# A chunked scan with a gated feed-forward layer on one core: fewer dummy matmuls, a block's outputs in two steps, first block's splitting after the second block's attention

## The chip, the core and the metric

The kernel runs on one core of a Trainium2 chip. The core has a matmul engine (TensorE; in the profile PE for its matmuls and PEld for its weight loads) and three engines that work on whole tiles: VectorE (DVE), ScalarE (ACT) and GpSimd (POOL). SyncE (SP) starts the DMA transfers here. Each engine runs its own list of instructions in order and waits on semaphores for the others. Matmuls read SBUF, the on-chip memory, and write PSUM, which has eight banks; DVE and ACT read PSUM and write back to SBUF. The metric is the device time of one execution in microseconds (us), the median of several.

## What is computed

Attention with a decay over 768 positions in 4 batches and 8 heads, in chunks, with a state carried from chunk to chunk; its output, as 3,072 tokens of 256 features, goes through a gated feed-forward layer of width 1,536.

```python
for c in range(nc):
    cum = np.cumsum(la, axis=-1)
    L = np.exp(cum[:, :, :, None] - cum[:, :, None, :]) * causal
    y_intra = np.einsum('bhij,bhjd->bhid', (Cc @ Bc^T) * L, xc)
    y_inter = np.einsum('bhin,bhnd->bhid', Cc, state) * np.exp(cum)[:, :, :, None]
    y[:, :, sl] = y_intra + y_inter
    state = decay_full[:, :, None, None] * state + np.sum(Bx, axis=2)
...
g = x @ w_gate
silu = g * (1.0 / (1.0 + np.exp(-g)))
val = x @ w_val
return (silu * val @ w_out)
```

## The kernel before

The 768 positions are cut into six blocks of 128 (k = 0 to 5), and each block into two pieces of 64. A block of all four batches is 512 tokens, the width of one PSUM bank and of the large matmuls.

**Attention of a block.** The decays of a block are loaded into `L` and `E` and turned into products by scans on DVE (`scan_j`, `scan_n`; for three batches of block 0 the rows are first spread over the partitions by TensorE, tiles `a0_0` to `a2_1`). DVE weighs `xb` (`weigh_b`) and, late, `bc` (`weigh_c`). TensorE forms the sums of each piece (`sums`, tiles `st`) and the scores (`scores`, tiles `S`). DVE multiplies scores and decays (`mix`, which writes `L`; its steps are named ("M", k, p)) and steps the states (`T`). `outputs` then forms the block's result in four PSUM banks `y`: for each batch `values` (16 matmuls y<-L,xb) and `carried` (8 matmuls y<-bc,T). In the trace each such f32 matmul is two records with two weight loads. Block 0 has its own order: `values` for all batches in two groups, then `carried`.

**Feed-forward of a block.** For each f of 12 slices of the width, `gate_val` gives the gate (m = 0) and the value (m = 1), tiles `gv`; ACT takes the silu of the gate into `sg`, DVE multiplies it by the value (`product`), the result is split into a high and a low half (`hh` by `hid_high`, `hl` by `hid_low`), and `project` adds it to two banks `po`, which are copied out and stored. Block 0 uses unsplit f32 copies (`xf`) and unsplit weights for its `gv`: two matmuls each, four records. From block 1 on x and the weights are split into halves too (`xh`, `xl`; `wg0h`, `wg0l`, ...), six matmuls each.

**Weights.** They arrive as 64-bit numbers. Each of 18 pieces (12 of gate and value, `wg`, 6 of the output, `wo`) goes through `w_magnitude`, `w_range`, `w_rest`, `w_shift`, `w_sign` and `w_round` on ACT and DVE. The rounded f32 weight (the trace's CUSTOM_DVE write to `wg0w`) serves block 0. `w_high` and `w_low` split it for the later blocks.

**Dummies.** `idle` issues three bf16 matmuls of a tile of ones by itself into a spare bank, `rest0` or `rest1`. The list `IDLE` (L856) has one number for each call, its rank, in two groups: 23 calls in the first and 24 in the second, whose first call needs block 0's first mix.

**What sets the order.** Nothing is issued in the order of the code. `add` enters each step with an engine or a choice of engines, a cost, a rank (when it is due), what it needs, which buffers it takes and uses, and what it gives. `Plan.order` then simulates the engines with these costs and issues, each time, a step that can start first, and among those the one with the lowest rank. `Plan.clocked` lets planned matmuls take twice as long in a window of 3.4133 us when the window before it had less than 1.28 us of matmuls. The order that comes out is fixed in the program. At run time an engine never passes a waiting instruction, so a step planned too early holds what stands behind it, and a dummy is run whether or not it is needed. The order's buffers bind as well: four PSUM banks for `gv` and `po`, four for attention and dummies, 21 tiles `sg` (shared by the rounded `wg` weights and the products), four raw weight tiles, and one each of `L`, `E`, `bc`, `xb`.

In the code before, the outputs of a block are one step, added at L801:

```python
add("PE", 3.2, do(outputs, k), z + 11, need, takes=[("at", i) for i in y], uses=[L, *uses], gives=("y", k), kind="f", slack=SLACK)
```

`w_high` is added at L715 and `hid_high` at L833. Since all operations pass through a helper, the profile puts them on L192; its tile names tell them apart.

Of the kernel before, what the change touches and what calls it, by code (L numbers as in the profile page):

```python
# [17 lines left out]
BATCH, H, S, D, N = 4, 8, 768, 32, 16  # L18
# [9 lines left out]
NP = H // 2  # L28
NF = DFF // P
# [13 lines left out]
class Plan:  # L43
# [6 lines left out]
    WINDOW, AWAKE = 3.4133, 1.28  # L50
# [12 lines left out]
    def add(self, engine, cost, run, rank, needs=(), takes=(), uses=(), gives=None, kind=None, lag=0.0, rows=1.0, slack=0.0):  # L63
        engines = [(engine, cost)] if cost is not None else engine
        self.ops.append(Op(engines, run, rank, needs, takes, uses, gives, kind, lag, rows, slack))
# [37 lines left out]
    def clocked(self, t, cost, rows):  # L103

        while cost > 1e-9:
            w = int(t / self.WINDOW + 1e-9)
            rate = 1.0 if self.active.get(w - 1, 0.0) >= self.AWAKE else 0.5
            d = min(cost / rate, (w + 1) * self.WINDOW - t)
            self.active[w] = self.active.get(w, 0.0) + d * rate * rows
            cost -= d * rate  # L110
            t += d
        return t
# [90 lines left out]
def scan_moe_kernel(ctx: ExitStack, tc, aj, an, bc, xb, wgv, wo, cst, sel, out):  # L203
# [279 lines left out]
    def outputs(k):  # L483
        for b in range(BATCH):
            values(k, (b,), (0, 1))
            carried(k, b)
# [179 lines left out]
    def do(f, *a):  # L666
        return lambda *e: f(*a, *e)
# [4 lines left out]
        dict(SP=5.2, Act=3.0, DVE=1.0, PE=1.5, Pool=2.0, **{"-": 0.7}),  # L672
    )
    add = plan.add
# [29 lines left out]
    for i in range(NW):  # L704
# [10 lines left out]
        add([("Act", 0.6), ("DVE", 0.36)], None, do(w_high, i), r - 2.7, [("round", i)], gives=("wh", i))  # L715
# [9 lines left out]
    for k in range(NB):  # L725
        r = due(k)
# [19 lines left out]
        if not k:  # L746
# [14 lines left out]
            add("DVE", 0.35, clip_n, -1.4, ["an"], gives="clip_n")  # L761
            add("DVE", 1.17, do(scan_n, 0), -1.3, ["clip_n"], gives=("E", 0))
# [36 lines left out]
        if k:  # L799
            need = [*(("M", k, p) for p in range(NP)), ("ce", k), *steps]  # L800
            add("PE", 3.2, do(outputs, k), z + 11, need, takes=[("at", i) for i in y], uses=[L, *uses], gives=("y", k), kind="f", slack=SLACK)  # L801
# [14 lines left out]
    for k in range(NB):  # L816
        xs = [(t, k, i) for t in ("xh", "xl") for i in range(2 * K)]
        for f in range(NF):
# [14 lines left out]
            add([("Act", 0.6), ("DVE", 0.36)], None, do(hid_high, k, f), r, [("pr", k, f)], takes=[("hh", h)], uses=[t], gives=("hh", k, f))  # L833
# [22 lines left out]
IDLE = [-9.0] * 8 + [-3.8, -3.3, -2.8] + [-1.2 + 0.1 * i for i in range(12)], [15.0 + 0.5 * i for i in range(24)]  # L856
# [56 lines left out]
```

## Time and profile before

| | us |
|---|---|
| median of 3 runs | 369.84 |
| lowest, highest | 366.42, 373.3 |
| the profiled execution | 368.33 |
| its span, first to last instruction | 366.6 |
| mean granted TensorE clock in it | 0.995 |

The span is 1.7 us shorter than the time of the execution it belongs to. Three views of the profile are used further down. The chain of work that ended last starts from the last instruction and goes back, at each step, to what released it; its rows give start, length and tile, and "issue" is time in which the engine waited for nothing that the profile shows. The timeline lists what each engine ran, with the wait before it in brackets. The windows give each engine's busy time and instruction count in a stretch, with the granted clock and the DMA rate. A matmul's recorded duration overlaps its neighbours', so lengths of a stage are taken from start to start.

### The profile page before, as it was taken

The page shows a single profiled execution, that of the slowest core. Times are in us where ns is not written, and L with a number is a line of the kernel's source. Part 1 is how long each engine was busy: PE and PEld are TensorE (multiplying, and loading weights), DVE is VectorE, ACT ScalarE, POOL GpSimd, SP SyncE. Part 2 cuts the span into 40 slices and gives each one's busy share as a digit, 9 for nine tenths or more (in the row PEclk, how much of TensorE's full clock was granted, in tenths as well). Part 3 has the DMA queues.
Part 4 walks back from the last instruction along what each step waited for, and adds up shares of the span by engine and source line. Part 5 has one row for each costly group of instructions (what it writes and reads, how often), then busy time and mean ns, then how long its engine had stood idle before and what let it go on. Part 6 is the DMA issues. An engine that isn't in the chain of part 4 may idle for free.

```text
span 366.6 us, 7587 instructions
## 1 busy us (share of the span) xinstructions
PE 357.5 (98%) x3293; PEld 276.0 (75%) x3293; DVE 231.0 (63%) x409; ACT 127.0 (35%) x225; POOL 0.8 (0%) x6
## 2 busy tenths in 40 slices
PE   8989999999999999999999999899999899999996
PEld 6855445488877888877788877688878688888895
DVE  3899999989999693663367554359345334352241
ACT  3275684444234543121342221323312133221242
POOL 0000000000000000000000000000000000000000
PEclk9999999999999999999999999899999999999999
DMA  6749742880101921000550000570100000100001
GB/s 181 283 134 285 240 146 87 237 224 2 58 2 46 207 95 59 0 3 2 172 119 25 35 2 2 143 148 2 57 0 3 4 0 2 57 0 2 0 0 59
DMA packets 8737, 28.62 MB, mean 78 GB/s; under 512 B 1008, under 2 KB 1912, under 8 KB 8064
## 3 DMA queue, kind: packets, MB, share of 16 engines
q1 hardware_dynamic: 8704, 28.14, 26.3%
q8 instruction: 26, 0.43, 0.5%
q14 instruction: 7, 0.06, 0.0%
HBM read 24.79 MB, written 3.35 MB: 77 GB/s over the span
## 4 chain that ended last, share of the span: by engine, by line
PE 94%; DVE 3%; issue 2%; ACT 0%; ACTq 0%
PE gv L192 55%; PE po L192 27%; PE y L192 5%; PE rest L192 3%; PE S L192 2%; PE a L192 1%; PE st L192 1%; DVE L L192 1%; DVE wo4w L192 0%; DVE sg L192 0%; DVE wo3w L192 0%; DVE wo4l L192 0%; DVE wo3l L192 0%; ACT wo5w L192 0%; ACT wo4w L192 0%
## 5 line engine op out<-in xcount | busy, mean ns | idle before, releaser
L192 DVE TENSOR_TENSOR sg<-gv,sg 128x512 f32<-128x512 f32 x72 | 49.4, 687 | 83.0 <-PE gv L192 80.6
L192 ACT ACTIVATE sg<-gv 128x512 f32<-128x512 f32 x72 | 42.9, 596 | 108.8 <-PE gv L192 108.6
L192 DVE TENSOR_TENSOR hl<-sg,hh 128x512 fp32r<-128x512 f32 x72 | 48.6, 685 | 17.5 <-ACT hh L192 17.0
L192 ACT CAST hh<-sg 128x512 fp32r<-128x512 f32 x56 | 34.9, 622 | 46.1 <-PE po L192 35.6
L192 DVE TENSOR_TENSOR_SCAN L<-L,dj 128x520 f32<-128x520 f32 x21 | 25.8, 1233 | 1.0 <-DMA L<-clipped 1.0
L192 DVE TENSOR_TENSOR L<-S,L 128x512 f32<-128x512 f32 x24 | 15.4, 682 | 2.2 <-PE S L192 2.2
L192 PEld LDWEIGHTS <-unit 128*128 128x128 bf16 x141 | 11.5, 122 | 4.9 <-issue 3.7
L192 PE MATMUL y<-L,xb 64*32 64x64 f32 x768 | 11.7, 223 | 3.2 <-issue 3.2
L192 ACT COPY ob<-po 128x512 f32<-128x512 f32 (+1 forms) x13 | 7.2, 555 | 21.3 <-PE po L192 20.8
L192 PE MATMUL rest<-unit 128*128 128x128 bf16 x141 | 12.9, 263 | 1.0 <-DVE warm L192 1.0
L192 PEld LDWEIGHTS y<-L,xb 64*32 64x32 f32 x768 | 7.6, 105 | 5.8 <-issue 3.9
L192 PE MATMUL y<-bc,T 32*64 32x64 f32 x352 | 10.2, 229 | 1.2 <-issue 1.2
L192 PEld LDWEIGHTS y<-bc,T 32*64 32x64 f32 x352 | 7.2, 131 | 4.5 <-issue 2.7
L192 PE MATMUL po<-hh,wo0h 128*128 128x512 f32 (+1 forms) x26 | 9.9, 382 | 0.0
L192 DVE CAST xh<-y 128x256 fp32r<-128x256 f32 x8 | 3.0, 418 | 10.9 <-PE y L192 10.9
L192 PE MATMUL po<-hh,wo2h 128*128 128x512 f32 (+1 forms) x26 | 9.8, 378 | 0.0
L192 PE MATMUL po<-hl,wo5h 128*128 128x512 f32 (+1 forms) x26 | 9.8, 377 | 0.0
L192 ACT CAST xh<-y 128x256 fp32r<-128x256 f32 x12 | 3.8, 379 | 17.1 <-PE y L192 17.1
L192 PE MATMUL po<-hl,wo0h 128*128 128x512 f32 (+1 forms) x26 | 9.7, 374 | 0.0
L192 PE MATMUL po<-hh,wo1h 128*128 128x512 f32 (+1 forms) x26 | 9.7, 373 | 0.0
L192 PE MATMUL po<-hl,wo3h 128*128 128x512 f32 (+1 forms) x26 | 9.7, 373 | 0.0
L192 PE MATMUL po<-hh,wo0l 128*128 128x512 f32 (+1 forms) x26 | 9.7, 373 | 0.0
(285 smaller groups left out, 800.5 us busy)
## 6 DMA issues: line engine op xcount, KB each, us to landing
L<-clipped SPq DMA_DIRECT2D x10, 520.0 KB
xb<-in_xb SPq DMA_DIRECT2D x6, 768.0 KB, 12.0
bc<-in_bc SPq DMA_DIRECT2D x6, 512.0 KB, 3.8
out<-ob SPq DMA_DIRECT2D x11, 256.0 KB, 2.2
E<-clipped SPq DMA_DIRECT2D x5, 260.0 KB
wg0r<-in_wgv SPq DMA_DIRECT2D x1, 512.0 KB
wg1r<-in_wgv SPq DMA_DIRECT2D x1, 512.0 KB
wg2r<-in_wgv SPq DMA_DIRECT2D x1, 512.0 KB, 9.9
```

The costliest lines, as they stand in the source:

```text
L192: ins = getattr(self.engine, name)(*a, **k)
```

## The change

There are four edits.

1. `IDLE` keeps 8 calls (24 matmuls) ahead of everything and 14 (42 matmuls) for gaps, with a rank of 1000: they are planned only where nothing else could start. 141 dummies become 66.
2. The outputs of blocks 1 to 5 are two steps of two batches each. Between them stands a step on an engine that exists only in the plan, "~", with a cost of 2.6, so that the plan puts other matmuls there. The first half takes the four banks, the second gives the block's result and frees its buffers.
3. For block 0, `hid_high`, and for the twelve `wg` weights `w_high`, need the last mix of block 1, ("M", 1, NP - 1). Low halves follow high halves, so they move too.
4. Inside the plan, matmuls ahead of 17 us always count as slow, and the ranks of `clip_n` and `scan_n` of block 0 are later.

```diff
-    WINDOW, AWAKE = 3.4133, 1.28
+    WINDOW, AWAKE, COLD = 3.4133, 1.28, 17.0
...
-            rate = 1.0 if self.active.get(w - 1, 0.0) >= self.AWAKE else 0.5
+            rate = 1.0 if t >= self.COLD and self.active.get(w - 1, 0.0) >= self.AWAKE else 0.5
...
-    def outputs(k):
-        for b in range(BATCH):
+    def outputs(k, bs):
+        for b in bs:
             values(k, (b,), (0, 1))
             carried(k, b)
...
-        add([("Act", 0.6), ("DVE", 0.36)], None, do(w_high, i), r - 2.7, [("round", i)], gives=("wh", i))
+        later = [("M", 1, NP - 1)] if i < NF else []
+        add([("Act", 0.6), ("DVE", 0.36)], None, do(w_high, i), r - 2.7, [("round", i), *later], gives=("wh", i))
...
-            add("DVE", 0.35, clip_n, -1.4, ["an"], gives="clip_n")
-            add("DVE", 1.17, do(scan_n, 0), -1.3, ["clip_n"], gives=("E", 0))
+            add("DVE", 0.35, clip_n, -1.15, ["an"], gives="clip_n")
+            add("DVE", 1.17, do(scan_n, 0), -1.12, ["clip_n"], gives=("E", 0))
...
-            add("PE", 3.2, do(outputs, k), z + 11, need, takes=[("at", i) for i in y], uses=[L, *uses], gives=("y", k), kind="f", slack=SLACK)
+            add("PE", 1.6, do(outputs, k, (0, 1)), z + 11, need, takes=[("at", i) for i in y], uses=y, gives=("y", k, 0), kind="f", slack=min(k - 0.5, 2.5))
+            add("~", 2.6, lambda: None, z, [("y", k, 0)], gives=("pause", k))
+            add("PE", 1.6, do(outputs, k, (2, 3)), z + 11, [("pause", k)], uses=[L, *uses], gives=("y", k), kind="f")
...
-            add([("Act", 0.6), ("DVE", 0.36)], None, do(hid_high, k, f), r, [("pr", k, f)], takes=[("hh", h)], uses=[t], gives=("hh", k, f))
+            add([("Act", 0.6), ("DVE", 0.36)], None, do(hid_high, k, f), r, [("pr", k, f)] + ([] if k else [("M", 1, NP - 1)]), takes=[("hh", h)], uses=[t], gives=("hh", k, f))
...
-IDLE = [-9.0] * 8 + [-3.8, -3.3, -2.8] + [-1.2 + 0.1 * i for i in range(12)], [15.0 + 0.5 * i for i in range(24)]
+IDLE = [-9.0] * 8, [1000.0] * 14
```

Three places of the resulting order follow. The first is TensorE's list behind the first 24 dummies, in the front of the program (`a0_0` and so on are the spread decay rows, `unit` the tile of ones), before:

```order
L192 MATMUL a0_0_138<-rows_86,pick_82 128x260
L192 MATMUL a0_1_140<-rows_86,pick_82 128x260
L192 MATMUL a1_0_146<-rows_86,pick_82 128x260
L192 LDWEIGHTS unit_81
L192 MATMUL rest0_110<-unit_81 128x128
```

and now:

```order
L192 MATMUL a0_0_138<-rows_86,pick_82 128x260
L192 MATMUL a0_1_143<-rows_86,pick_82 128x260
L192 MATMUL a1_0_151<-rows_86,pick_82 128x260
L192 MATMUL a1_1_159<-rows_86,pick_82 128x260
L192 MATMUL a2_0_161<-rows_86,pick_82 128x260
L192 MATMUL a2_1_165<-rows_86,pick_82 128x260
L192 MATMUL S0_0_169<-Cz0_140,bc0_92 64x128
L192 MATMUL S0_1_170<-Cz0_140,bc0_92 64x128
```

The nine dummies in the middle of the a are gone, and so are the 36 between the scores and the sums of block 0; scores, sums, values and carried part now follow one another. Then 21 dummies stand ahead of the first gv (27 before), none between gv0_0 and gv0_3 (45 before), 9 ahead of gv0_7 and 12 ahead of block 1's scores.

The second place is TensorE's list around the outputs of block 3 (y3_0 to y3_3 are its four banks), before, from the end of the fourth batch:

```order
L192 MATMUL y3_2_1967<-bc3_1488,T3_1494 64x64
L192 MATMUL y3_3_1968<-bc3_1488,T3_1494 64x64
L192 MATMUL gv2_9_0_2066<-xh2_979,wg9h_887 128x512 x2
L192 MATMUL gv2_9_0_2066<-xh2_979,wg9l_966 128x512 x2
L192 MATMUL gv2_9_0_2066<-xl2_980,wg9h_887 128x512 x2
L192 MATMUL gv2_9_1_2086<-xh2_979,wg9h_887 128x512 x2
L192 MATMUL gv2_9_1_2086<-xh2_979,wg9l_966 128x512 x2
L192 MATMUL gv2_9_1_2086<-xl2_980,wg9h_887 128x512 x2
L192 MATMUL gv2_10_0_2100<-xh2_979,wg10h_909 128x512 x2
```

and now, from the end of the second batch:

```order
L192 MATMUL y3_2_1892<-bc3_1433,T3_1439 64x64
L192 MATMUL y3_3_1893<-bc3_1433,T3_1439 64x64
L192 MATMUL gv2_9_0_1943<-xh2_889,wg9h_836 128x512 x2
L192 MATMUL gv2_9_0_1943<-xh2_889,wg9l_894 128x512 x2
L192 MATMUL gv2_9_0_1943<-xl2_890,wg9h_836 128x512 x2
L192 MATMUL gv2_9_1_1950<-xh2_889,wg9h_836 128x512 x2
L192 MATMUL gv2_9_1_1950<-xh2_889,wg9l_894 128x512 x2
L192 MATMUL gv2_9_1_1950<-xl2_890,wg9h_836 128x512 x2
L192 MATMUL y3_0_1890<-L3_1437,xb3_1458 32x64
L192 MATMUL y3_2_1892<-L3_1437,xb3_1458 32x64
```

The twelve matmuls of gv2_9 stood behind all four batches and now stand between the second and the third. Blocks 4 and 5 read alike; in block 1 the pair gv0_10 stands there, in block 2 the projections of f = 4 and 5.

The third place is ACT's list from the copies of block 0's result on (`sg` is a silu, `hh` and `wg0h` are high halves), before:

```order
L192 COPY xf_131<-y0_1_338 128x4x64
L192 CAST wg0h_442<-wg0w_238 128x512
L192 ACTIVATE sg0_0_456<-gv0_0_0_445 128x512
L192 CAST wg1h_461<-wg1w_306 128x512
L192 CAST wg2h_466<-wg2w_375 128x512
L192 ACTIVATE wg4r_429<-wg4r_429 128x512
L192 CAST hh0_0_494<-sg0_0_456 128x512
L192 ACTIVATE sg0_1_504<-gv0_1_0_488 128x512
```

and now:

```order
L192 COPY xf_131<-y0_1_260 128x4x64
L192 ACTIVATE sg0_0_406<-gv0_0_0_393 128x512
L192 ACTIVATE wg4w_411<-wg4r_361 128x512
L192 ACTIVATE sg0_1_432<-gv0_1_0_420 128x512
L192 ACTIVATE sg0_2_448<-gv0_2_0_439 128x512
L192 ACTIVATE wg5w_454<-wg5r_408 128x512
L192 ACTIVATE sg0_3_461<-gv0_3_0_450 128x512
```

The casts to high halves left this stretch. They now follow block 1's mix: wg0h to wg11h on ACT, then hh0_0, with the low halves of wg0 to wg6 on DVE ahead of block 1's xh and xl and those of wg7 to wg11 behind them. On DVE the rest of the stretch reads as before, less the two low halves of weights and the two of hidden values that stood ahead of block 1's scans. On SP one load moved: bc2 now goes out ahead of L2 and E2.

More of the change, by code (lines that the diff above doesn't have):

```diff
@@ L671, in scan_moe_kernel @@
         dict(mm=4, at=4, L=1, E=1, bc=1, xb=1, Cz=1, T=2, tmp=2, raw=4, w=1, x=2, hh=HB, sg=SG, ob=2),
-        dict(SP=5.2, Act=3.0, DVE=1.0, PE=1.5, Pool=2.0, **{"-": 0.7}),
+        dict(SP=5.2, Act=3.0, DVE=1.0, PE=1.5, Pool=2.0, **{"-": 0.7, "~": 0.0}),
     )
```

## The prediction

> **What bounds the kernel now.** I read the page's engine shares first, then the chain of work that ended last in order of time, then single stretches of it. Columns of the chain: start in us, length in us, what ran.
>
> ```profile
> PE 357.5 (98%) x3293; PEld 276.0 (75%) x3293; DVE 231.0 (63%) x409; ACT 127.0 (35%) x225; POOL 0.8 (0%) x6
> ...
> 26.32 0.67 PE rest L192 x12
> ...
> 35.42 0.50 PE rest L192 x9
> ...
> 113.50 3.10 PE y L192 x192
> ...
> 170.93 2.73 PE y L192 x173
> 173.66 1.05 issue
> 174.71 0.60 PE y L192 x17
> ...
> 229.69 1.22 issue
> ...
> 231.75 10.01 PE gv L192 x36
> ...
> 287.36 0.93 issue
> ...
> 289.10 8.38 PE gv L192 x36
> ```
>
> TensorE carries the chain from the first gate/value matmul (gv) to the last projection (po), so time comes off only where it does something useless or nothing. There are four such places. (1) The front, until gv starts. (2) Dummy matmuls (rest) between the first gv: 45 in five pieces, of which the first and the last are shown, at 0.67/12 = 0.056 us each. (3) Inside the output stage (y) of blocks 3, 4 and 5 it stands still for 1.05, 1.22 and 0.93 us, 3.20 in all, while nothing in the profile is waited for ("issue"). Block 2's y has no such gap (3.10 us). (4) After the second gap, 36 gv take 10.01 us instead of 8.38: 1.63 us more.
>
> The next rows are windows: from:to, length, busy us and number of instructions of PE, PEld, DVE, ACT, POOL, granted clock, DMA share, GB/s. The three bounds 174.5, 230.5 and 288.0 lie inside gaps or just behind one. The first line is the instruction queue: packets, MB, share.
>
> ```profile
> q8 instruction: 26, 0.43, 0.5%
> ...
> 174.50:230.50 56.00, 54.99 (x510) 44.19 (x509) 31.36 (x53) 15.84 (x28) 0.00 (x0) 1.00 0.21 58
> 230.50:288.00 57.50, 56.44 (x509) 45.54 (x509) 30.08 (x50) 15.97 (x28) 0.00 (x0) 0.97 0.23 56
> ...
> 231.90:235.30 3.40, 3.40 (x9) 2.62 (x9) 1.90 (x6) 1.10 (x4) 0.00 (x0) 0.50 0.62 193
> 235.40:238.80 3.40, 3.40 (x16) 2.77 (x15) 0.69 (x1) 1.76 (x3) 0.00 (x0) 1.00 0.93 228
> ```
>
> From gap to gap TensorE issues 510 + 509 = 1,019 and 509 + 509 = 1,018 instructions: equal strides. PE has 3,293 + 3,293 = 6,586 in all and the instruction queue moved 26 packets: 253 instructions each, and four packets make a stride. I therefore take a gap for the wait for the next packet of code. Such a wait needs a whole packet to be used up faster than the next one comes. In y 192 matmuls with 192 loads take 3.10 us, so 253 instructions last 2.0 us; in gv (36 + 36 in 8.38 us) they would last 29 us. Only a y stage uses code fast enough, and only where a whole packet lies within it.
>
> The half clock (0.50) fills one window of 3.4 us right behind the gap in block 4; the next has 1.00. I read it as a consequence of a thinly used window before it, which the gap helped to make.
>
> **The front and the clock.** Rows of the timeline: start, length, engine, operation, in brackets the wait before it.
>
> ```profile
> 1.05 2.74 PE L192 MATMUL rest<-unit 128*128 128x128 bf16 x24 [1.05 <-DVE warm L192]
> ...
> 3.72 2.97 PE L192 MATMUL a<-rows,pick 8*128 8x260 f32 x6
> ...
> 10.59 2.01 PE L192 MATMUL S<-Cz,bc 32*64 32x128 f32 x64
> ...
> 13.22 3.88 PE L192 MATMUL rest<-unit 128*128 128x128 bf16 x36
> ...
> 15.61 1.28 DVE L192 TENSOR_TENSOR L<-S,L 128x512 f32<-128x512 f32 x2
> ...
> 18.44 0.42 DVE L192 TENSOR_TENSOR T<-st,cs 128x256 f32<-128x256 f32 x1 [1.22 <-PE st L192]
> ...
> 21.32 1.51 PE L192 MATMUL rest<-unit 128*128 128x128 bf16 x24
> 21.33 0.68 DVE L192 CUSTOM_DVE_ANT_0 wg0w<-wg0r,wg0w 128x1024 uint16<-128x1024 uint16 x1
> 21.93 0.41 DVE L192 COPY xf<-y 128x256 f32<-128x256 f32 x1
> ...
> 22.67 3.65 PE L192 MATMUL gv<-xf,wg0w 128*128 128x512 f32 x8
> ...
> 52.35 1.21 PE L192 MATMUL S<-Cz,bc 32*64 32x128 f32 x64
> ```
>
> A dummy takes 3.88/36 = 0.108 us at 13.22 and 1.51/24 = 0.063 at 21.32, and the same 64 S matmuls 2.01 us at 10.59 and 1.21 later. So the front runs at half rate until the 36 dummies have kept TensorE full for 3.9 us; the first 24 (2.74 us) did not suffice. [...]
>
> Now the front of the changed order. The six a go back to back, the 64 S follow, and the sums (st) come straight behind them, not behind 36 dummies. DVE has the same work up to the last mix; the clip that moves ahead of two scans costs nothing if its load is in by 7.3, when before ran it. So the mix ends at 16.9 as now. DVE's wait of 1.22 us for st goes, and the rounding of weight 0 ends near 20.8 instead of 22.0. Its two xf copies (one now) stand behind two more splitting steps and end near 22.2. On TensorE y runs cold: 160 records at 3.10/192 are 2.6 us, times 2.01/1.21 are 4.3. The half that waits for the last two mixes (64 records, 1.7 us) and the carried part (32, 0.9) end at 19.6 to 20.2. Then stand 21 dummies, cold 21 x 0.108 = 2.3 us. gv starts at 22.4 against 22.67: **-0.3** (ends -1.0 and +0.6, for y0 warmer or colder). The gap of 1.22 us in this y hid behind the rounding and is worth nothing.
>
> Dense work starts at 20.2. If between 2.7 and 3.9 us of it are needed, plus up to a window for the phase, full clock comes between 22.9 and 26.3, and gv loses half of what lies behind 22.4: 0.25 to 1.95 us. I take **+0.9**, below the middle, since y counts a little. [...]
>
> **The first block's stage.**
>
> ```profile
> 42.68 3.60 PE L192 MATMUL gv<-xf,wg5w 128*128 128x512 f32 x8
> 46.12 3.60 PE L192 MATMUL gv<-xf,wg6w 128*128 128x512 f32 x8
> ...
> 55.30 3.60 PE L192 MATMUL gv<-xf,wg8w 128*128 128x512 f32 x8
> 58.83 0.46 PE L192 MATMUL y<-L,xb 64*32 64x64 f32 x32
> ...
> 61.93 3.70 PE L192 MATMUL gv<-xf,wg9w 128*128 128x512 f32 x8
> 65.47 3.60 PE L192 MATMUL gv<-xf,wg10w 128*128 128x512 f32 x8
> ...
> 71.93 1.03 PE L192 MATMUL gv<-xh,wg0h 128*128 128x512 f32 x2
> ...
> 43.78 0.68 ACT L192 ACTIVATE wg7w<-wg7r 128x512 f32<-128x512 f32 x1 [1.82 <-DMA wg7r<-in_wgv]
> ...
> 36.00:72.00 36.00, 36.00 (x393) 17.28 (x392) 35.60 (x69) 22.35 (x42) 0.00 (x0) 1.00 0.58 182
> ```
>
> The 45 dummies go: **-2.52**. New are 9 and 12 dummies later: 21 x 0.056 = **+1.2**. A pair of gv takes 46.12 - 42.68 = 3.44 us, next to y 58.83 - 55.30 = 3.53 and 65.47 - 61.93 = 3.54: 0.1 us for each change of kind, so **+0.2** for the second half of y. DVE is as full as TensorE here (35.60 of 36.00 us), so what TensorE gains holds only if DVE needs no more. Before the mix DVE loses two low halves of weights and two of hidden values, 4 x 0.6 = 2.4 us. That is the cover: weight 7, in SBUF at 43.8, needs about 4 us of other and own steps on DVE and is ready near 47.8, and TensorE asks for it near 48.1. On the late side, between the mix and the first split matmul (gv<-xh), DVE has some 10 us of steps, TensorE two halves of y and four gv, 2 x 1.65 + 2 x 3.44 = 10.2 us, and x-low is needed 0.9 us later still. I cost the delay at 0 (ends -0.3 and +2). ACT, 22.35 of 36 us busy, takes the high halves. Stage: 49.26 - 2.52 + 1.2 + 0.2 + 0.9 = 49.0; gv<-xh starts at 22.4 + 49.0 = 71.4 instead of 71.93.
>
> **The later blocks.** Each half of y is 96 of the 192 records, 1.55 us, and 12 gv or po (2.7 us) lie between: a packet of code now spans at least 1.9 us of y and those 2.7, well over the 3.2 us that pass between two packets where it stalls (the stretch of a gap and a y packet, 1.2 + 2.0). Gaps: **-3.20**. No window of 3.4 us can be thin then: **-1.63**. Four more pairs of changes of kind: **+0.8**. The second half frees the block's buffers 2.7 us later, so the next loads go out later; from block 3 on they have most of a block's 56 us. Block 2's are the near ones:
>
> ```profile
> 65.48 1.10 SPq L192 DMA_DIRECT2D L<-clipped  x2
> ...
> 78.15 1.24 DVE L192 TENSOR_TENSOR_SCAN L<-L,dj 128x520 f32<-128x520 f32 x1 [0.97 <-DMA L<-clipped]
> ...
> 108.01 1.17 PE S L192 x59
> ```
>
> L2 is sent at 65.48 and its first scan waits for it until 78.15. With y1 ending near 68 it is sent at 68, behind bc2, which now stands ahead of it and E2 on SP (the one change of SP's order), and is scanned near 80.6. DVE's list from there to the copy of st2 that S2 waits for (108.01, after DVE's T in the chain) has 3.1 us less in it, since the last steps of the fifth projection weight moved behind it. S2 comes near 107.4, as much earlier as gv<-xh: 0 (ends -0.5 and +2).
>
> Sum: -0.5 - 3.20 - 1.63 + 0.8 = -4.5. The span of 366.6 becomes 362.1, and with the 1.7 us around it (368.33 - 366.6) 363.8 us. That is 1.2% under the profiled run and 1.6% under the median, 369.84, whose runs spread from 366.42 to 373.3; as an estimate, steps of half-clock windows (1.6 us) would make that spread.
>
> **Rivals.**
> - *The gaps stay.* If they aren't code, or code comes no sooner, splitting y only adds its 0.8. [...] Time: 363.8 + 3.2 + 1.63 = 368.6.
> - *The front gains more.* The clock comes early (-0.7), xf sets gv's start at 22.0 (-0.4), and block 2's S no longer waits for DVE (-0.5): 362.2.
> - *The first block loses.* Clock at its late end (+1.1) and weight 7 or 8 late on DVE (+1): 365.9.
> - *Slower than before: the delayed low halves pile up.* All twelve now stand behind the mix, 12 x 0.6 = 7.2 us. If DVE reaches the first x-low later than TensorE reaches gv<-xh, each us is lost. For it: DVE has no idle time. Against: seven of them lie under the two gv pairs. Unhidden, they give 363.8 + 7.2 = 371.0; it passes the median once DVE is 6 us late there.
>
> **How the numbers follow.** Forecast 0.60; gaps stay 0.09; front gains more 0.15; first block loses 0.12; pile-up 0.04. The range leaves out the pile-up, most of the gaps and the far end of the front's gain: 361.4 to 367.0. About 2% is what a measurement of this kernel can tell from no change: 362.4 and 377.2 against the median. Under 362.4 lie most of the front's case, and a fifth of the forecast, since the median itself moves: 0.28. Above 377.2: 0.02. Between: 0.70.
>
> **What would show it.** Right: no "issue" inside y of blocks 2 to 5, y in two pieces of about 1.55 us, granted clock 1.00 from about 26 us on, gv starting near 22.4, gv<-xh near 71.4. Wrong: an idle TensorE before a gv of block 0 with DVE's rounding as releaser; half clock behind 26 us; TensorE waiting for x-low before gv<-xh; gaps that only moved.

## The result and the profile after

| | before | after |
|---|---|---|
| median, us | 368.64 | 364.69 |
| lowest, highest | 365.73, 373.3 | 361.19, 367.79 |
| executions | 14 | 14 |
| the profiled execution, its span | 368.33, 366.6 | 362.94, 361.1 |

The ratio of after to before is 0.9898, with an interval of 0.9863 to 0.9932. A second series gave 363.26 against 367.67, ratio 0.9877 (0.9835 to 0.9919). The medians hold all executions; the ratios and their intervals, here and below, leave out executions disturbed by a slower state. The change makes the kernel about 1% faster, clear of noise but less than the 2% named in the prediction, which gave that outcome 0.70. The forecast was 363.8.

The page of the kernel after, engine shares and granted clock in 40 slices:

```profile
PE 350.4 (97%) x3218; PEld 268.4 (74%) x3218; DVE 231.7 (64%) x410; ACT 127.1 (35%) x224; POOL 0.8 (0%) x6
...
PEclk9589999999999999999999999999999999999999
```

TensorE issues 75 matmuls fewer (3,293 before) and is busy 7.1 us less; its share of the span is 97% (98% before). Half clock (0.50 in the windows) is on record only in the front.

The chain of work of the kernel after, around the outputs of block 3 (start, length, what ran):

```profile
168.79 1.81 PE gv L192 x8
170.61 1.57 PE y L192 x94
172.18 2.95 PE gv L192 x12
175.13 1.55 PE y L192 x96
```

The two halves of y take 1.57 and 1.55 us with 12 gv in 2.95 us between, and no "issue". Blocks 4 and 5 read alike, and no y of blocks 1 to 5 has a gap.

Where the span went is read from stages, each from the start of one block's first gv to that of the next. The first stage starts with the "dense" gv: the third gv matmul of block 0, from which on gv runs without a wait for xf. Windows of the kernel before (from:to, length, busy us and instructions of PE, PEld, DVE, ACT, POOL, clock, DMA share, GB/s):

```profile
23.58:71.93 48.35, 48.35 (x460) 23.91 (x459) 47.08 (x91) 29.26 (x53) 0.00 (x0) 1.00 0.66 203
71.93:143.88 71.95, 71.88 (x610) 58.28 (x609) 62.68 (x110) 27.56 (x48) 0.00 (x0) 1.00 0.31 84
143.88:200.06 56.18, 55.13 (x537) 44.34 (x536) 31.35 (x53) 15.87 (x29) 0.00 (x0) 1.00 0.21 58
200.06:257.92 57.86, 56.64 (x538) 45.73 (x536) 31.35 (x53) 15.94 (x29) 0.00 (x0) 0.97 0.23 56
257.92:313.64 55.72, 54.79 (x505) 44.38 (x504) 23.54 (x40) 14.62 (x27) 0.00 (x0) 1.00 0.03 11
```

The same windows of the kernel after:

```profile
23.45:70.72 47.27, 47.27 (x435) 22.92 (x436) 45.36 (x89) 25.87 (x48) 0.00 (x0) 1.00 0.63 200
70.72:143.56 72.84, 72.44 (x611) 58.04 (x609) 65.03 (x113) 31.78 (x56) 0.00 (x0) 1.00 0.34 88
143.56:198.50 54.94, 54.94 (x538) 44.38 (x536) 31.55 (x53) 15.85 (x29) 0.00 (x0) 1.00 0.22 59
198.50:253.44 54.94, 54.94 (x538) 44.37 (x536) 30.77 (x52) 15.86 (x29) 0.00 (x0) 1.00 0.22 59
253.44:308.21 54.77, 54.77 (x505) 44.17 (x504) 24.34 (x42) 14.64 (x27) 0.00 (x0) 1.00 0.03 11
```

By gv<-xh the kernel is 1.21 us ahead (70.72 against 71.93). The next stage, gv of block 1 to gv of block 2, gives 0.89 back (72.84 against 71.95). The three stages that hold y of blocks 3, 4 and 5 gain 1.24, 2.92 and 0.95, and in them TensorE is now busy all the time. The sum is 5.43 us, nearly the whole difference of the spans (366.56 and 361.13).

What was given back is a wait. The timeline of the kernel after, VectorE and TensorE in block 1's projections:

```profile
133.20 0.29 DVE L192 TENSOR_TENSOR xb<-xb,L 128x128 f32<-128x128 f32 x1 [1.83 <-DMA xb<-in_xb]
...
135.28 0.50 PE L192 MATMUL po<-hl,wo3h 128*128 128x512 f32 x1 [0.41 <-DVE hl L192]
```

VectorE stands 1.83 us at the weighting of block 3's xb until that load lands; the low halves (hl) of block 1 stand behind it on VectorE, and TensorE then waits 0.41 us for one of them.

The front hardly gained. Rows of its timeline:

```profile
8.80 0.43 DVE L192 TENSOR_SCALAR L<-L 128x512 f32<-128x512 f32 x1 [3.59 <-DMA L<-in_aj]
...
9.89 1.23 PE L192 MATMUL a<-rows,pick 8*128 8x260 f32 x2 [3.66 <-DVE L L192]
...
22.63 0.76 DVE L192 COPY xf<-y 128x256 f32<-128x256 f32 x2
...
23.45 1.12 PE L192 MATMUL gv<-xf,wg0w 128*128 128x512 f32 x2 [0.42 <-DVE xf L192]
```

The clip of L, now ahead of the scans of a, waits 3.59 us for its load, the scans wait behind it, and TensorE's last a wait 3.66 us for the scans to free their banks. The very first gv starts at 21.93 (22.67 before), but the next ones wait for the second half of xf, and the dense gv starts at 23.45 (23.58 before).

### The profile page after: what moved, and what is told of

It is laid out like the page before. It is cut to its first block, busy times and chain, and to the rows that moved or that the text cites. A ratio compares the mean times of both kernels' runs of the same rounds, so it can differ in the third digit from the quotient of the medians.

```text
span 361.1 us, 7445 instructions
## 1 busy us (share of the span) xinstructions
PE 350.4 (97%) x3218; PEld 268.4 (74%) x3218; DVE 231.7 (64%) x410; ACT 127.1 (35%) x224; POOL 0.8 (0%) x6
## 4 chain that ended last, share of the span: by engine, by line
PE 74%; DVE 12%; DMA 6%; issue 2%; ACT 1%; SPq 1%; DVEq 0%; ACTq 0%
PE gv L192 47%; PE po L192 21%; PE y L192 3%; DMA xb<-in_xb 3%; DMA L<-clipped 3%; DVE L L192 2%; DVE sg L192 1%; PE S L192 1%; DVE hl L192 1%; SPq L192 1%; PE st L192 1%; DVE wo2w L192 1%; DVE wo5w L192 1%; DVE wo3w L192 1%; DVE E L192 1%
## 5 line engine op out<-in xcount | busy, mean ns | idle before, releaser
L192 PE MATMUL po<-hh,wo3h 128*128 128x512 f32 (+1 forms) x26 | 9.8, 377 | 0.0
L192 ACT ACTIVATE Cz<-bc,cs 128x512 f32<-128x512 f32 x10 | 6.7, 718 | 8.7 <-DMA bc<-in_bc 8.7
L192 PE MATMUL po<-hh,wo3l 128*128 128x512 f32 (+1 forms) x26 | 9.7, 374 | 0.0
L192 PE MATMUL po<-hl,wo2h 128*128 128x512 f32 (+1 forms) x26 | 9.7, 373 | 0.0
L192 PE MATMUL po<-hl,wo4h 128*128 128x512 f32 (+1 forms) x26 | 9.7, 373 | 0.0
```

The costliest lines, as they stand in the source:

```text
L192: ins = getattr(self.engine, name)(*a, **k)
```

## The experiments

The theory (C in the expectations): the lost time in y is the wait for the next packet of code; it falls in whichever block has a whole packet inside an unbroken y, so what decides is how many instructions stand ahead of y. The main rival: the gain comes from the dummies taken out and from the front, and the gaps are something of the blocks themselves. All medians stand in the table at the end of this section.

### One step again

The kernel after with y in one step; edits 1, 3 and 4 stay.

```diff
-            add("PE", 1.6, do(outputs, k, (0, 1)), z + 11, need, takes=[("at", i) for i in y], uses=y, gives=("y", k, 0), kind="f", slack=min(k - 0.5, 2.5))
-            add("~", 2.6, lambda: None, z, [("y", k, 0)], gives=("pause", k))
-            add("PE", 1.6, do(outputs, k, (2, 3)), z + 11, [("pause", k)], uses=[L, *uses], gives=("y", k), kind="f")
+            add("PE", 3.2, do(outputs, k, range(BATCH)), z + 11, need, takes=[("at", i) for i in y], uses=[L, *uses], gives=("y", k), kind="f", slack=SLACK)
```

> The changed kernel with the outputs of a block in one step again. Theory C (a gap is the wait for the next packet of code, 256 instructions; it opens where a whole packet lies inside y): the 150 instructions that are gone ahead of it move the packet borders. By counting instructions, two borders now lie in y of blocks 1 and 2 (58 and 314, 68 and 324 instructions into its 384) and one in blocks 3, 4 and 5 (245, 190, 200). So gaps of about 1 us in blocks 1 and 2, at about four fifths of y, and none in 3, 4 and 5; no pause costs 5 x 0.25 less, two gaps cost 2 x 1.3 more: 364.7 - 1.2 + 2.6 = about 366, up to 368 if half-clock windows follow them. Rival S (a gap comes from an unbroken y of 384 instructions in the later blocks as such): gaps in 3, 4 and 5 as before, 368 to 369. Rival N (the split does nothing): no gaps anywhere, 363.5.

It took 363.39 us, ratio to before 0.9895 (0.9845 to 0.9944), about as the kernel after; the expected 366 was too high. From its timeline:

```profile
62.98 0.32 PE L192 MATMUL y<-L,xb 64*32 64x64 f32 x11
64.41 0.42 PE L192 MATMUL y<-L,xb 64*32 64x64 f32 x21 [1.11 <-issue]
```

And its window from the one gap to the other (columns as above):

```profile
64.00:115.80 51.80, 50.95 (x509) 38.61 (x509) 49.35 (x90) 24.46 (x44) 0.00 (x0) 1.00 0.30 83
```

The gaps are back, but in blocks 1 and 2 (1.11 and 0.78 us), where the count of instructions put them, and not in blocks 3, 4 and 5. Between them lie 509 + 509 matmuls and loads, the stride of the kernel before. The wait belongs to the place in the code, not to the block.

### Dummies of the same length in fewer instructions

The kernel before; the 23 calls of the first group issue one matmul of 384 columns in place of three of 128 (the tiles `unit` and `rest` are widened to match). The plan and the order stay; the count falls by 92 instructions.

```diff
-        for _ in range(3):
-            te.matmul(rest[n], unit, unit, start=True, stop=True)
+        wide = n == 0
+        for _ in range(1 if wide else 3):
+            m = 3 * P if wide else P
+            te.matmul(rest[n][:, :m], unit[:, :P], unit[:, :m], start=True, stop=True)
```

> The kernel before with one dummy matmul of 384 columns in place of three of 128 in the first group of dummies (69 become 23): the same plan, order and TensorE time, 92 fewer instructions ahead of everything from block 0's gv on. Theory C: two borders in y of blocks 1 and 2 (16 and 272, 9 and 265), one in 3, 4 and 5 (186, 132, 141): the three gaps leave blocks 3, 4 and 5 and two of up to 1.3 us come in blocks 1 and 2; 1 gap fewer, about 1 to 3 us under before: 366 to 368. Rival S: gaps stay in 3, 4 and 5, the time is that of before, 368.6.

It took 364.22 us, under the 366 to 368 expected, ratio 0.9891 (0.9853 to 0.993): a shift of the code by 92 instructions is worth as much as the whole change. It is not the front's doing: in the profile gv<-xh starts at 71.79 (71.93 before). The gaps in blocks 3, 4 and 5 are gone. That they would come back in blocks 1 and 2 was wrong: both have y of 192 matmuls in one piece, as the chain of block 1 shows:

```profile
58.76 3.10 PE y L192 x192
```

There the borders lie 14 and 8 instructions into y, counted in the trace, and the next 256 further on, still in y. Whether that is a rule is asked below, with thin dummies.

### Two steps alone

The kernel before with edit 2 alone (the lines above the other way round).

> The kernel before with the outputs in two steps, nothing else. Theory C: no gap in y of blocks 1 to 5 although every border stands where it stood in blocks 3 to 5, no half clock there: the three gaps, counted with the drain around them 1.28 + 1.54 + 1.25 = 4.1 us, and about two half-clock windows of 1.6 go, five pauses cost 5 x 0.25 = 1.2 and the later load of block 3 some 0.6: 368.6 - 4.1 - 1.6 x 1 to 2 + 1.8 = about 363.5 to 365. So nearly all of the gain is this edit. Rival S' (the gain is the front's): 367 to 369.

365.4 us, ratio 0.9944 (0.9916 to 0.9971): about half of the gain, and a little over the 363.5 to 365 expected. No gap in blocks 1 to 5, though the borders lie where they lay, so the pause does what it says; the stages with y of blocks 3 to 5 take 55.89, 54.92 and 54.73 us. In the profiled execution the rest is lost ahead of them: by a gap in block 0's y, which is not split (before has 1.22 us there),

```profile
20.81 0.57 PE L192 MATMUL y<-bc,T 32*64 32x64 f32 x23 [1.61 <-issue]
```

in the timeline, and by a half-clock window behind it, which before lacks:

```profile
21.82:25.24 3.42, 3.42 (x22) 2.39 (x19) 3.39 (x8) 0.54 (x2) 0.00 (x0) 0.50 0.63 180
```

The first gv starts at 23.43 (22.67 before) and gv<-xh at 73.79 (71.93). But in 8 of the 10 executions the mean clock is 0.998 or more, so no such window is on record in them, and their median is 365.2: the window doesn't explain the median, and what the others lost isn't in a profile.

### Fewer dummies alone

The kernel before with edits 1 and 4.

> The kernel before with the new list of dummies and the new planning of the clock and of block 0's scan, nothing else. Theory C: gaps move to blocks 1 and 2 as in the changed kernel with one step (borders 58 and 314, 68 and 324). The first block's stage loses 45 dummies (2.5 us) and keeps the early splitting; the front's clip waits for its load as in the changed kernel (about +1). About 366 to 368. Rival F (the front is where the changed kernel's time comes from): 364.5 or less.

362.75 us in only 4 executions, ratio 0.9866 (0.9811 to 0.992), under the 366 to 368 expected and where the rival had it. The gaps are where the count says: 0.88 us in block 1 and 0.67 in block 2.

```profile
62.10 0.32 PE L192 MATMUL y<-L,xb 64*32 64x64 f32 x11
63.30 0.42 PE L192 MATMUL y<-L,xb 64*32 64x64 f32 x21 [0.88 <-issue]
```

So fewer dummies alone bring as much as the whole change, within the intervals. They take 45 useless matmuls out of the first block's gv, and they shift the code by 150 instructions, so that three gaps and a half-clock window become two shorter gaps. The rival, that the time comes from the front, holds for a part: gv<-xh starts at 70.61, 1.32 us earlier than before, of 5.1 us by which the span is shorter.

### The changed kernel again, and without the delay

The second profile of the kernel after was to show what belongs to the kernel and what to one execution.

> The changed kernel once more, beside the three that follow. Its first profile has a front in which the clip of L0 waited 3.59 us for its transfer; the runs of the parts alone waited 2.0 to 2.2 there. Theory A (that wait is chance of one execution's transfers): this profile has a shorter wait, the first block's dense gv starts near 22.5 instead of 23.45, and the span is about 360.3. Theory B (it belongs to this kernel): again 3.3 to 3.8 us, 23.4 and 361.1. Either way: no gap in y of blocks 1 to 5, a pause of y that costs about 0.25 us in each, a wait of TensorE for hl in block 1's po near 135 us; median 363 to 365.5.

The other kernel is the kernel after without edit 3:

```diff
-        later = [("M", 1, NP - 1)] if i < NF else []
+        later = []
...
-            add([("Act", 0.6), ("DVE", 0.36)], None, do(hid_high, k, f), r, [("pr", k, f)] + ([] if k else [("M", 1, NP - 1)]), takes=[("hh", h)], uses=[t], gives=("hh", k, f))
+            add([("Act", 0.6), ("DVE", 0.36)], None, do(hid_high, k, f), r, [("pr", k, f)], takes=[("hh", h)], uses=[t], gives=("hh", k, f))
```

> Fewer dummies and two steps, without edit 3: the splitting of block 0 is not held back. Theory A (holding it back costs the late loads): the second half of block 1's y no longer pushes the xb load of block 3 later, the wait for hl near 135 us goes and block 1's step from its gv to block 2's gv is about 72.3 instead of 72.84; median about 0.5 below the changed kernel. Theory B (holding back gains what it was put in for, DVE free for block 1's scans): 0.5 to 1.0 above it, with waits of TensorE on DVE ahead of gv<-xh of block 1 (70.72 there). Theory C (neither): within 0.4 of it.

The second profile of the kernel after ran the front faster (dense gv at 22.0, gv<-xh at 69.58) and lost it all in block 1: its stage took 74.53 us. Its rows:

```profile
133.76 0.29 DVE L192 TENSOR_TENSOR xb<-xb,L 128x128 f32<-128x128 f32 x1 [1.99 <-DMA xb<-in_xb]
...
135.84 0.50 PE L192 MATMUL po<-hl,wo3h 128*128 128x512 f32 x1 [1.79 <-DVE hl L192]
```

The load was sent at 120.11 us (121.15 in the first profile), and the weighting that waits for it began at 133.76 (133.20): near the same time in both, so a TensorE that is earlier waits longer. Without the delay the median was 364.46, ratio 0.9918 (0.9877 to 0.9958), against 0.9877 (0.9835 to 0.9919) for the kernel after beside it: not told apart. Its profile has a wait in block 1's gv that looks like the one edit 3 might prevent, but VectorE's rows name the same culprit, xb's load, here block 2's:

```profile
84.01 0.29 DVE L192 TENSOR_TENSOR xb<-xb,L 128x128 f32<-128x128 f32 x1 [2.54 <-DMA xb<-in_xb]
...
87.22 0.73 PE L192 MATMUL gv<-xh,wg5h 128*128 128x512 f32 x2 [1.91 <-DVE sg L192]
```

What the delay is worth on top of the other edits stays open, within about one per cent.

### The clip of L later

The kernel after, with the clip of L held behind a scan of a.

```diff
-                    add("DVE", 0.35, do(clip_j, b), r - 0.5, ["aj"], gives=("clip", b))
+                    add("DVE", 0.35, do(clip_j, b), r - 0.5, ["aj", ("scan0", 1)], gives=("clip", b))
```

> The changed kernel with one rank of edit 4's consequence undone: the clip of L0 stands behind all but one of the scans of a again instead of ahead of six of them. Theory A (the wait of the clip for the transfer of L0 is on the path to the first gv): DVE's scans of a start on time, the mix ends 1 to 2 us earlier, the dense gv of block 0 starts near 22 instead of 22.5 to 23.5, median 0.7 to 1.5 below the changed kernel. Theory B (the path to the first gv is the weights' rounding and xf, which start behind it anyway): the gain in the front is below 0.4 and the median the same.

365.78 us, ratio 0.9945 (0.99 to 0.999): not better. The edit failed its purpose, since in the new order the clip of E came to stand ahead of four of the scans of a and waited instead. Rows of VectorE and TensorE:

```profile
9.97 0.43 DVE L192 TENSOR_SCALAR E<-E 128x512 f32<-128x512 f32 x1 [3.42 <-DMA E<-in_an]
...
15.61 0.68 PE L192 MATMUL st<-xb 64*32 64x64 f32 x32 [4.39 <-DVE xb L192]
```

It doesn't decide between its two theories. It shows that a clip ahead of the scans holds them for as long as its load is late, here 3.42 us.

### Thin dummies

Fewer dummies alone, with the first 24 matmuls of 128 columns cut into 52 of 59: nearly the same columns (3,068 for 3,072), 56 instructions more.

```diff
-        for _ in range(3):
-            te.matmul(rest[n], unit, unit, start=True, stop=True)
+        m = 59 if n == 0 else P
+        for _ in range(3 if n else 6 + i % 2):
+            te.matmul(rest[n][:, :m], unit, unit[:, :m], start=True, stop=True)
```

> Fewer dummies alone (edits 1 and 4), with the 24 matmuls of 128 columns at the start cut into 52 of 59: the same columns in 56 more instructions. By the count of instructions the borders of the packets of code then lie 2 and 258 instructions into block 1's y, 11 and 267 into block 2's, 188, 134 and 143 into the next three. Theory A (a gap comes only where TensorE runs through a whole packet inside y, and with a border within some 16 instructions of y's start the next packet was already asked for while y waited): no gap in any block, the two of 1.09 and 0.88 us of the kernel without this cut gone, span about 359.4, median about 361. Theory B (the borders at 258 and 267 gap as those at 314 and 324 did): gaps of about 1 us in blocks 1 and 2 again, 362.7.

No gap in any of blocks 1 to 5; y of block 1 is one piece again, with borders 2 instructions ahead of its start and 254 into it, counted in the trace:

```profile
61.53 3.10 PE y L192 x192
```

So the theory holds for the gaps in these blocks, with its condition made sharper: a border from 2 instructions ahead of y's start to 14 behind it did no harm at four places (two with wide dummies, two here), one 43 or more behind it did wherever the next lay in the same unbroken y. The transfers of code show the difference: at the four harmless places a packet starts 1.1 to 2.6 us ahead of y (here 60.35, with y from 61.53), ahead of a gap only 0.9 to 1.4 us behind y's start (172.34, with y from 170.93, in block 3 of the kernel before). Why it is sent for earlier there wasn't tried. The median, 363.99, ratio 0.9922 (0.9886 to 0.9958), did not fall to the expected 361: TensorE lost 1.1 us at 191.4 to a wait for hl, and the dense gv started at 23.59.

### The weighting of xb later

Now the suspected cost of block 1 by itself. The planner is told that xb's load takes longer, so that it puts the weighting later on VectorE; in the kernel after, and in the kernel with fewer dummies alone.

```diff
-        add(*q, load(load_xb), z - 6 if k else -6, late + gate("xb") + behind("xb"), takes=[("xb", XB)], gives=("xb", k), lag=1.95)
+        add(*q, load(load_xb), z - 6 if k else -6, late + gate("xb") + behind("xb"), takes=[("xb", XB)], gives=("xb", k), lag=5 if k >= 3 else 1.95)
```

> The changed kernel with one number of the planner's changed: it is told that the load of xb of blocks 3 to 5 takes 5 us instead of 1.95, so that the first of the weightings of xb stands three low halves later on VectorE. Nothing else moves on TensorE, the borders of the code lie as before. Theory A (the low halves of block 1 stand behind a weighting that waits for xb's transfer, and TensorE waits for them: 1.65 us lost at 135.8 and 0.55 at 249.3 in the second profile of the changed kernel, 0.56 at 135.3 in the first): both waits go, the step from block 1's gv to block 2's gv comes down from 72.8 to 74.5 to 72.3, median 0.5 to 2 below the changed kernel's 363.3, at 361.5 to 362.8. Theory B (the low halves are late of themselves): TensorE waits for hl at the same place again and the median stays.

> Fewer dummies alone (edits 1 and 4) with the same number for xb. Theory A: the wait of TensorE for hl near 191 (1.2 to 1.3 us lost) goes, the gaps of 1.09 and 0.88 in y of blocks 1 and 2 stay, the step of block 2 comes down from 56.4 to about 55.2, median about 361.5. If theory A holds in both this kernel and the changed one, their difference is what the two steps and the delay are worth when neither is disturbed: by my reading of the parts the two steps save two gaps (about 1.4 us together) and cost five pauses of 0.25 (1.25), so within 0.5 us of one another.

In neither profile does TensorE wait for hl any more. With two steps it took 362.85 us, ratio 0.9866 (0.9815 to 0.9916); block 1's stage took 73.31 us, with 1.0 us of another wait of TensorE (for VectorE's T) in place of the 0.4 to 1.8 for hl. With fewer dummies alone it took 362.62, ratio 0.9877 (0.9835 to 0.9919), and the stage of block 2 54.72 instead of 56.40. The two are alike, as the expectation had it; its reason, that two steps save two gaps and cost five pauses, is a sum and no measurement.

### The delay alone

The kernel before with edit 3 alone.

> The kernel before with edit 3 alone: the last roundings of block 0's weights and the high halves of its hidden values wait for block 1's masks. TensorE's instructions are as many and in nearly the same order, so the three gaps stay at 3777, 4801 and 5825 instructions. Theory A (the delay is worth nothing here, as forecast at 0, ends -0.3 and +2): 368 and the stage steps of before within 0.3. Theory B (it frees VectorE for block 1's scans): gv<-xh of block 1 earlier than 71.9 by 0.5 or more. Theory C (the roundings come late for block 1's gv): waits of TensorE for the rounded weights behind 72, slower by up to 2.

Ratio 0.9995 (0.9946 to 1.0044): no difference. Its three gaps stand where those of before stand, 0.99, 1.23 and 1.48 us, at the same counts of instructions. gv<-xh starts at 70.41 instead of 71.93, more than theory A allows, but the dense gv already started 1.5 us earlier in this execution (22.06 instead of 23.58) and the first block's stage is 48.35 us in both, so theory B's gain isn't there.

### Both small edits together

Thin dummies and the later weighting, on fewer dummies alone.

> The two small edits that took single waits away, together, on fewer dummies alone: the starting dummies cut into 52 thin matmuls (no gap in y of any of blocks 1 to 5) and the weighting of xb put later (no wait for hl in po). Theory A (the losses add up along TensorE): against fewer dummies with the late weighting alone the gaps of 1.37 and 1.31 us in blocks 1 and 2 go, 1.0 and 1.0 us of lost time with them, span about 359, median 360.8 to 361.5, the lowest of all. Theory B (what is saved on TensorE before block 2 is waited for again on VectorE, since block 1's step is set by VectorE's scans and roundings): the step of block 1 stays at 72.3 to 73.1 with new waits in it, and the median at 362 to 363.

The profile is what theory A says: no gap in blocks 1 to 5, no wait for hl, a stage of 71.43 us for block 1, and the shortest span of all profiles, 359.7.

```profile
71.11:142.54 71.43, 71.43 (x610) 58.13 (x609) 62.54 (x109) 28.62 (x49) 0.00 (x0) 1.00 0.31 87
142.54:197.24 54.70, 54.70 (x538) 44.48 (x537) 31.36 (x53) 15.86 (x29) 0.00 (x0) 1.00 0.24 59
```

The median does not follow, and misses A's 360.8 to 361.5: 363.33 us, ratio 0.9908 (0.9874 to 0.9943), where the profiled execution took 361.48 and the others up to 365.75. No version is shown to be faster than the changed kernel. What the other executions lost isn't in a profile.

| kernel | median, us | ratio to before | gaps in y, of blocks 1 to 5 |
|---|---|---|---|
| after | 364.69 | 0.9898 (0.9863 to 0.9932) | none |
| after, again | 363.26 | 0.9877 (0.9835 to 0.9919) | none |
| y in one step | 363.39 | 0.9895 (0.9845 to 0.9944) | 1, 2 |
| wide dummies | 364.22 | 0.9891 (0.9853 to 0.993) | none |
| two steps alone | 365.4 | 0.9944 (0.9916 to 0.9971) | none |
| fewer dummies alone | 362.75 | 0.9866 (0.9811 to 0.992) | 1, 2 |
| after without the delay | 364.46 | 0.9918 (0.9877 to 0.9958) | none |
| clip of L later | 365.78 | 0.9945 (0.99 to 0.999) | none |
| thin dummies | 363.99 | 0.9922 (0.9886 to 0.9958) | none |
| after, xb weighted later | 362.85 | 0.9866 (0.9815 to 0.9916) | none |
| fewer dummies, xb weighted later | 362.62 | 0.9877 (0.9835 to 0.9919) | 1, 2 |
| delay alone | 369.37 | 0.9995 (0.9946 to 1.0044) | 3, 4, 5 |
| thin dummies, xb weighted later | 363.33 | 0.9908 (0.9874 to 0.9943) | none |

## Why the prediction was right, step by step

- *Gaps are waits for code, -3.20, and two steps remove them: right, and the term too small.* The shifted code moved the gaps by instruction count, three times to the very blocks that the count had said (y in one step, fewer dummies, and these with the later weighting). Measured from stage to stage the gaps cost more than "issue" showed. In the kernel after y and the 36 gv around it take 11.73 us, pause included; without a pause or a gap they are 3.10 + 8.38 = 11.48. In the kernel before they took 12.76, 14.65 and 12.73. Less 11.48 that is 1.28, 3.17 and 1.25, and without the half clock's 1.63 the gaps are 4.07 us. Of the difference of 0.87, 0.65 is the last matmul ahead of each gap, which the profile of the kernel before counts as busy for 0.22 us.
- *Half clock behind the second gap, -1.63: right for the profiled execution.* No window behind 20.93 us has it any more. That a thinly used window brings it was the prediction's reading; no run shows it (last section). Of 82 executions of the kernel before beside the experiments, the 23 with a mean clock of 0.994 to 0.996 (one window of 3.41 us at half, 0.5 x 3.41 / 366.6 = 0.005) have a median of 369.14 us, and the 22 with 0.999 or 1.000 one of 366.65. Of 24 executions of the kernel after, none lies at 0.994 to 0.996. This fits the estimate that such windows make the spread, though 2.5 us is more than the 1.7 that one of them costs. The other 37 executions can't be sorted so, since the mean can count the front's half clock too (13.65 us of it make the 0.981 of the kernel after). The 22 without such a window had nothing to gain by this term.
- *Changes of kind, +0.2 for each block: right.* 11.73 - 11.48 = 0.25 per block.
- *45 dummies of block 0 out, -2.52; 21 as fillers, +1.2; a clock that comes late, +0.9: the first two right, the last wrong.* From dense gv to gv<-xh the stage took 48.35 before and 47.27 after, -1.08. The terms without the clock give -2.52 + 1.2 + 0.2 = -1.12. The clock was at full at 20.93, before gv began. The step that failed is "Dense work starts at 20.2": the y of block 0, at half rate, and the first dummies behind it filled the window 17.52 to 20.93 completely (3.41 of 3.41 us), and the clock was released at its end. How much dense work that takes no run shows; the 2.7 to 3.9 us, and up to a window more, were an estimate from the rows of the kernel before.
- *The front, -0.3: -0.13 by the dense gv, -0.74 by the first gv, which the prediction meant.* Its condition, that the load of L is in by 7.3, failed: the clip waited until 8.80, and the mixes ended at 17.97 instead of 16.9. The condition was also too weak: VectorE was free for the clip at 8.80 - 3.59 = 5.21, so a load in at 7.3 would have held it as well. Nine profiles with this order of clip and scans have the wait, 1.39 to 3.59 us long; that of the kernel before has none. TensorE's wait of 3.66 us for its last a lies under the same wait; the second half of xf, which stands behind the late mixes in VectorE's list, then held gv for 0.42 us.
- *The delay costs nothing: right as far as measured*, by the run with edit 3 alone.
- *Later loads cost nothing for block 3 and on: wrong.* "From block 3 on they have most of a block's 56 us" holds for the loads' use in block 3, but not for the place of the weighting, which the plan puts among block 1's low halves. Here it cost 0.56 us in the first profile (0.79 from start to start where 0.23 is usual) and 1.95 in the second (2.18 less 0.23). It is not the two steps' alone: with fewer dummies alone the wait came a block later, 1.2 us at 191.0.
- *The sum, -4.5 in the span: -5.43.* Larger gaps (-0.87) and no late clock (-0.9) outweigh the waits of block 1. That these errors partly cancelled is luck; the median, 364.69, lies 0.9 above the forecast, where the profiled execution, 362.94, lies as much below it.
- *What the sum gave to edit 2: wrong.* The prediction credited edit 2 with the whole -4.83 of gaps and half clock; edits 1 and 4 without it, or 92 instructions less, remove them from blocks 3 to 5 as well. By the prediction's own terms the kernel with y in one step would take 363.8 + 4.83 - 1.0 (five changes of kind) = 367.6 us; it took 363.39. So the mechanism, a wait for code, was right, and that the time of the whole change came out near the forecast is in part luck, since the dummies taken out had already moved the gaps.

The rival "the gaps stay" fell, since the gaps moved with the count of instructions. Most crossings from one block of 256 instructions to the next do pass without a wait: 22 of 26 in the kernel before, all 25 in the kernel after. In blocks 1 to 5 one does not (0.67 to 1.48 us) where the whole block ahead of it lies in the same unbroken y, unless that block begins at y's very start. "The front gains more" gave 362.2: its early clock came, its early xf did not. "The first block loses" and the pile-up did not come: between the dense gv and block 2's scores TensorE shows no wait for a weight, for x-low or for VectorE's T, and these scores start at 106.29 (107.50 before). What no rival held is that the dummies' number by itself moves the gaps.

## What to carry to other kernels

Here the "issue" gaps in runs of small matmuls, with equal counts of instructions between them, were waits for code. Where a profile looks like this, before restructuring, count instructions modulo 256 (the gaps of the kernel before stand 1,024 = 4 x 256 apart) and see whether fewer or wider ones ahead of the place already move the border out of it; and when a change of the front seems to help late stages, check whether it only moved a border. Where an engine that runs in order holds a step that waits for a transfer, look at what stands behind it: time won ahead of such a step is waited for again, as block 1 did here with up to 1.8 us.

## What was not expected of the hardware

The instruction transfer is seen directly. In the kernel before, the queue's one packet in the 1.2 us ahead of the first gap (transfers from 172.2 to 173.4 us):

```profile
q8 instruction: 1, 0.02, 5.0%
```

It runs from 172.34 to 173.30, and TensorE goes on at 174.71, 1.41 us after it ended. Counted in order of start, TensorE's matmuls, loads and semaphore instructions ahead of the one that goes on are 3,777 here, 4,801 and 5,825 in the other two gaps: each time 193 over a multiple of 256. The same remainder stands at all 12 gaps of blocks 1 to 5 in the profiles of this case, and TensorE goes on 1.2 to 1.6 us after a packet of this queue ended. The 256 instructions ahead of the first gap's end start at 171.51: 3.20 us lie between two borders, 3.71 and 3.41 in the other two gaps. A packet that an unbroken y used up in less was waited for in these profiles, but for those whose border lay at y's very start. That is so in blocks 1 to 5. In block 0 shorter gaps stand at the same remainder although the border ahead lies further back: with fewer dummies and the later weighting TensorE stands 0.73 us ahead of 17.08, 6.25 us behind that border, and the packet had started only 3.8 us behind it. Why it came so late isn't shown.

The recorded changes of the clock lie whole windows of 3.41 us apart: at 16.82, 231.86 (63 windows later) and 235.27 us in the kernel before, at 3.86, 7.28 and 20.93 in the kernel after. TensorE's busy time in a window does not decide by itself. Four windows at full clock: the first of the kernel before, the second of the delay alone, both followed by half clock; the third of fewer dummies with the later weighting, the fourth of the kernel after without the delay, both followed by full clock:

```profile
228.45:231.86 3.41, 2.19 (x113) 1.64 (x106) 0.13 (x1) 0.18 (x1) 0.00 (x0) 1.00 0.00 0
...
4.42:7.83 3.41, 3.32 (x21) 2.23 (x19) 2.28 (x5) 1.31 (x2) 0.00 (x0) 1.00 0.83 234
...
61.31:64.72 3.41, 2.25 (x100) 1.60 (x98) 2.55 (x6) 0.47 (x2) 0.00 (x0) 1.00 0.50 149
...
85.58:88.99 3.41, 1.77 (x8) 1.47 (x9) 3.41 (x6) 1.30 (x3) 0.00 (x0) 1.00 0.02 5
```

The second, lost with 3.32 us, holds mostly the a, whose matmuls use 8 rows; the fourth, kept with 1.77, holds gv alone, with 128 rows. What decides isn't shown. In the front of the kernel after:

```profile
3.86:7.28 3.42, 2.37 (x10) 1.69 (x10) 0.70 (x1) 1.31 (x2) 0.00 (x0) 1.00 0.87 200
...
10.69:14.10 3.41, 2.84 (x81) 1.84 (x80) 3.41 (x9) 0.00 (x0) 0.00 (x0) 0.50 1.02 397
14.10:17.52 3.42, 2.07 (x100) 1.60 (x102) 3.42 (x7) 3.23 (x6) 0.00 (x0) 0.50 0.74 290
17.52:20.93 3.41, 3.41 (x133) 2.91 (x121) 3.41 (x10) 2.79 (x7) 0.00 (x0) 0.50 0.21 62
20.93:24.34 3.41, 2.96 (x21) 1.58 (x19) 3.41 (x8) 0.00 (x0) 0.00 (x0) 1.00 0.42 127
```

Here the clock was released at 3.86, behind the 24 dummies at the start (2.74 us), where the prediction had read from the kernel before that they don't suffice; it was lost again at 7.28. These busy times are modelled.

The clock column has a trap: ahead of its first recorded change a profile can read 1.00 at half rate. In the kernel before that change is at 16.82 us; the window from 13.41 to 16.82 reads 1.00, yet a dummy takes 3.88/36 = 0.108 us there, against 0.060 at 21.39 (1.45/24). So a mean of 1.00, as in the second profile of the kernel after, does not show a fast front, and the 0.995 of the kernel before counts its slow front as full. What the front's half clock costs can't be told from the means.
